# Writing the memory readout in runs of 64 elements, with a new instruction order, in a fused two-branch attention kernel

## The chip, the cores and the metric

The kernel runs on one core of one Trainium2 chip. The metric is the device time of one execution in microseconds (us); lower is better. Five engines run side by side, each working through its own list in order: TensorE (PE in the profile, with its weight loads as PEld), VectorE (DVE), ScalarE (ACT), GpSimd (POOL) and SyncE (SP, which here only starts DMAs). An instruction starts when the ones ahead of it on its engine have gone and the semaphores it waits for have been raised.

## The reference, cut to what matters

There are 2048 tokens, a model width of 640 and 32 heads of 20 features. Two attention branches, A and B, are mixed by a gate per token.

```python
# branch B, for each of 4 segments s of 512 tokens, per head
logits = qs @ ks.T * scale + mask          # causal inside the segment
a_dot  = softmax(logits) @ vs
num    = phi(qs) @ M                       # M, z: sums over the segments before
den    = phi(qs) @ z + 1e-6
o      = g * (num / den) + (1 - g) * a_dot # g = sigmoid(beta), per head
M, z   = M + phi(ks).T @ vs, z + phi(ks).sum(rows)
# branch A: phi_k = softmax features of k, kv = phi_k.T @ v, z = sum of phi_k
o      = (phi_q @ kv) / (phi_q @ z + 1e-6)
# result: gate = sigmoid(x . gate_w)
out    = gate * (oA @ A_wo) + (1 - gate) * (oB @ B_wo)
```

The division `num / den` is what the change rewrites. In the first segment M and z are zero, so the kernel computes it for segments 1 to 3 only: 12 token tiles of 128 tokens.

## The kernel before, in words

Tokens stand in 16 tiles of 128, or 4 segments of 512. Branch B's projections (line 627) give q and k with features on the partitions, and SyncE copies and transposes them through DRAM. The attention of a segment runs in 8 steps of 4 heads (b_step): scores on PE (L754), exponentials on ACT (L763), causal masks on POOL (L767), then the product with v (L795). Branch A's key side (a_k: L894, L901, L907 to L909) and running sum of features (L949) fill the first half of the program, its query side (a_q: L1003, L1008, L1020, L1055, L1060, L1064) and the output product (final: L1083, L1084) the second.

The memory readout sits in b_out. For each of the 12 token tiles PE forms numerator and denominator for all heads in one PSUM tile of two banks, 16 heads to a bank, 21 fp32 words per head: 20 of the numerator and the denominator behind them (L858, L859). VectorE takes the 32 denominators out (L864), inverts them (L867), and then, once per bank, multiplies 16 heads by 20 features with the inverse of their head (L869) and writes bf16 into an SBUF tile `mo`. A DMA transposes `mo` into `moT` (L468), and L877 adds `moT` to the other half of the output `oP`. `mo` is laid out as (c b h d), c being 5 groups of features and d 4 features within a group, because `oP` has its rows in that order; so the 320 elements of one L869 lie in 5 runs of 64.

Nothing in the program decides the order at run time. A table, ORDER, lists all operations in the order in which they are recorded; each engine's list is that order cut down to its own operations. CHOICE says, for the operations that two engines could do (mostly copies out of PSUM: ACT at L606 or VectorE at L607), which one does, and WHERE gives each tile its PSUM bank or SBUF slot. A tile that takes over a bank waits until the last reader of the bank's former tile is done. NSPIN is the number of idle matmuls (L1095) that the table places where it likes.

Of the kernel before, what the change touches and what calls it, by code (L numbers as in the profile page):

```python
# [36 lines left out]
om 3o p5 3p ow ox 47 7z os ph 4l 7s 4n ot 3a 4i 4m 7k 4j 17 7t p8 4o p9 4p 48 p0 oi oj 4r p1 19 4q dc 4u pq ou 4v pi p6 4w pr oy 4x 7l dd p7 oz pa ps
54 6z 70 7u 56 4s 55 oq f 4t 7v 57 dk 72 or p2 58 50 4y 51 qh 52 pj qi pk 4z pb 5c dl 73 53 59 5d pd pc 71 5e di 5v 5a pl pm 7o pn dj 74 pe pf 8t da
16 5x 5w 5l 5n pg 7p 5m po 85 8r 5o pv q1 75 db 5g q2 5i 10o 76 77 q6 5h pp 5j pw q7 q8 qb bx 5y 1f 5z 5f 5r qe 5k by 5t pt qf pu qc py 5s 5u qg 5p 67
pz q0 69 68 82 8u 4k 5q bw qd 60 8a 61 8s 6c 10p bz q9 8b 6d 8c px 63 6e 64 dg 65 q3 qa 6m 6o do 6f 6n 6a dp q4 dh ho hr q5 r1 8v qj qk 66 r2 r3 qs r4  # L40
6i r5 qt 8d 6b 6k 8e ds ql 6j 8f 6g qu 6h qv 90 c0 qm qn 6p qw dt 6l 1e hs qo 92 91 qp c1 qq c2 qr 8w 8x hp 6q qx 83 8g 8y 1d 8h 8i c4 rp rq qy rr 8z
6r 6s 95 96 dq qz dr 97 r0 rh 9f r9 ri 93 rj 9h 84 88 62 c3 87 89 ru 9g 8j rv 1c 8k 98 rk ra c5 dm 8l rl 94 rb 9i 9b 9c 9d 10q rm 86 9j rn 99 dn r6 c6
j8 rw 9a j9 a6 sk a7 r7 9e ro re rf 3q 9k j2 a8 9w sl a9 sm rc 9y rs 6t j3 9l 9x hq ht rd sf rt a2 sg sp a3 a4 e2 e3 e4 rg r8 s0 9n s3 s4 s5 s6 a5 10r
s2 1b 9p rx s1 rz aa 9r 9o 9t 9z 5b ry 79 s7 s8 t0 s9 sa 9s 9u ss t1 sq j4 9q t2 9m st sb su t5 t6 sx ab ax ac 1o j5 9v sc ay sd se sr a0 az t7 sy sn
a1 sz so sh e5 si e6 e7 ai sv ak sw de sj aj te at b0 j6 au av t3 ad j7 t4 ae hu ag jc df ja dw tf af tg b1 du th ti dv an ao hv tz tb ap jd aq tc aw
hw jb t8 e8 ta e9 ea t9 b2 td tj dx b3 ah tk b9 al tl tm ba u6 bb b5 u0 b7 b6 u1 b8 c7 u7 u3 u2 u4 u8 u9 1p 1a ua am uc dy ub ar 1q 1v 1x 1y 1w 1z 20
78 c8 bc c9 ud hx ue be tv bf bg as je eb tt jf u5 bo uf ec bq hy bp 3r ed ug bd bk tw bm bh bi bj bl hz el ei br ca i0 bn jg i1 es eu et tr bs ee jh
uh ui bt bu ju jv uj f3 f4 f5 jx jy jw 7a eo eq 8m uk e0 um ep uo un ev 3s ji jz ex ez ts tn ey k0 k1 k2 f6 ew ul 7b jj to 8n f0 8o up tp er 8p cq f7
ej cr cs ct f9 cu f8 d2 d3 7c d4 d5 d6 fa e1 f1 fj ck f2 7d fk fl fb dz cl cm cn co tx tu k3 cv fc tq k4 fy ur k5 fz g0 ef uq 7e jk fu fw v7 b4 em jl
v8 va bv fd v9 v2 cb v3 v4 ty fv ux 7f v5 uy 7h v0 cp us vc vb jm ce uz v1 cc vl vf vm vd vg vn ut vo 7g ve cd g1 vi cf cw fx vh uu vj uv vk vp cx cg  # L50
zf vq vr uw g2 cy d0 ka zg cz vs d7 ch d1 ci en i2 fo fp fq fr ek zc ff vt zd kd vu v6 fg fh fi zl zm jn g3 g4 vv gl gn vw vy gm w0 vx eg zi d8 cj d9
zj eh gp wr ii gr ij ik gq ws vz w1 wu wv wt ww jp ic id fe x0 x1 wx x2 wy wo wz ie ig fm fn fs iu wp wq im if il gf gh gg kb ft gs iv iw iy ix w3 go
ga gc w2 gb x3 x4 g6 g7 jo js gi in wj w9 g8 w4 wk wl wm w5 gt ze we ih g9 wa w6 w7 y9 ya yb y0 gu wc wf y6 wh wb y1 k6 y2 gx gv gy wn gz wg zx h1 kc
zy gd y7 y8 ge h0 gj gk w8 h2 h3 x5 h4 h6 h7 wd x6 hg wi hh h5 hi hj x7 h8 jt x8 zo hc y3 hd zk h9 ha zp kv he zu kw ke kf kx kz hb x9 i6 hk zv y4 y5
l1 l0 hf hl ky hm kp kq xb yc kr ks kk kl jr zr km yd l2 gw l3 kg ye l4 kh ki kn zq hn zs xc lb iz jq lc ld l7 l9 l5 l8 ko kj xa kt g5 la ku i3 i5 i7
lg lh lm lo zz li le i4 xd lq lr ls lf ln lj lt lp xe xf yf l6 yg lk mh mj mi i8 lu md mf me lv m7 m8 m9 m2 m4 m3 lw mk ml ly m0 lz i9 mg k7 ma mm m5
# [7 lines left out]
012345671014530143501034035310301053401354130100220132001210012313223010233001103231132200126327101642110267010435001200310260313321401321241305100262
310403031521012313202031230103203160207210230030103413521200111214331010211321340232110023213001201030100113221103201020132033220332023023131200232304
567010530100000530241025103410230023200332000031011260710122230021132331002041005210607114500136371000042310030812332034031302116004071514567212010130
000041063201340182004512303245032250031112260126270014201076021610201020601021600011230030000213003232003120300223820013030221306120101232003518021733
# [1105 lines left out]
```

## Time and profile before

| | us |
|---|---|
| median of 3 runs (338.68 to 341.3) | 340.35 |
| the profiled execution | 340.44 |
| its span, first to last instruction | 338.9 |
| mean granted TensorE clock | 0.919 |
| PE busy in the span | 293.3 |
| VectorE busy | 255.5 |
| ScalarE busy | 247.3 |
| GpSimd busy | 121.5 |

The profiled execution is the one that all rows come from; 1.5 us of its time lie around the span. Busy time of PE is modelled from the starts of pipelined matmuls. [...] The chain of waits is followed back from the last instruction: at each step to the instruction that released it, or to the one before it on its engine.

### The profile page before, as it was taken

The numbers are of one execution on the slowest core, as the hardware profiler recorded it, in microseconds if no ns is written. First come the engines' busy times: TensorE is split into PE (matmuls) and PEld (weight loads), VectorE is DVE, ScalarE is ACT, GpSimd is POOL, SyncE is SP. The second block draws the span as 40 slices with busy tenths as digits, with TensorE's granted clock in tenths as the row PEclk, the third lists the DMA queues.
The fourth block names the chain that finished last, engine by engine and source line by source line (L and its number), as shares of the span: only waits on it lengthen the run. The fifth ranks groups of instructions, "written<-read, shape, count | busy, mean of one in ns | idle before, by whom it ended". The sixth has DMA issues, their size and how long they took to land.

```text
span 338.9 us, 7011 instructions
## 1 busy us (share of the span) xinstructions
PE 293.3 (87%) x2882; PEld 152.0 (45%) x2882; DVE 255.5 (75%) x394; ACT 247.3 (73%) x323; POOL 121.5 (36%) x135
## 2 busy tenths in 40 slices
PE   2999999999989999999984999956988667695996
PEld 2354544565455464454542454424534223352653
DVE  2457587998999998999978987696552325989970
ACT  4476698989989999999995668774699989740001
POOL 4002733329645857843422104203142455330000
PEclk9999999999999999999998799995999855767899
DMA  7999470043136301061064776542762541397462
GB/s 218 247 213 206 61 153 3 22 68 71 33 53 123 79 10 42 33 151 41 21 184 128 201 148 92 124 128 45 106 166 75 168 144 48 88 193 173 80 183 90
DMA packets 72271, 37.38 MB, mean 110 GB/s; under 512 B 55184, under 2 KB 69168, under 8 KB 72240
## 3 DMA queue, kind: packets, MB, share of 16 engines
q1 hardware_dynamic: 71488, 36.08, 47.1%
q10 hardware_dynamic: 656, 0.82, 0.7%
q8 instruction: 23, 0.38, 0.5%
q0 software_dynamic: 96, 0.04, 0.2%
q14 instruction: 8, 0.07, 0.1%
HBM read 14.01 MB, written 12.10 MB: 77 GB/s over the span
## 4 chain that ended last, share of the span: by engine, by line
PE 53%; DVE 26%; ACT 12%; DMA 7%; issue 1%; SPq 0%; ACTq 0%
PE ps L627 9%; PE ps L1083 9%; DVE mo L869 8%; ACT expT L763 7%; PE ps L894 6%; DVE acc L949 4%; PE ps L754 4%; PE ps L1055 4%; PE ps L1003 4%; PE ps L795 3%; PE ps L649 3%; DVE z L907 3%; DMA stk<-in_B_wk_dram 2%; PE ps L1084 2%; ACT ej L763 2%; DMA acc<-acc 2%
## 5 line engine op out<-in xcount | busy, mean ns | idle before, releaser
L763 ACT ACTIVATE expT<-ps 128x1024 bf16<-128x1024 f32 x128 | 123.8, 1031 | 16.4 <-PE ps L754 15.6
L767 POOL TENSOR_SCALAR_AFFINE_SELECT expT<-expT 128x512 bf16<-128x512 bf16 x96 | 71.9, 760 | 119.8 <-ACT expT L763 105.4
L627 PE MATMUL ps<-xT,WB 128*128 128x512 bf16 x200 | 50.7, 388 | 1.0 <-DVE xT L607 0.6
L767 POOL TENSOR_SCALAR_AFFINE_SELECT ej<-ej 128x1024 bf16<-128x1024 bf16 x16 | 19.6, 1225 | 55.5 <-ACT ej L763 52.4
L763 ACT ACTIVATE ej<-ps 128x1024 bf16<-128x1024 f32 x32 | 31.4, 1030 | 6.8 <-PE ps L754 6.7
L869 DVE TENSOR_TENSOR mo<-ps,cs 128x320 bf16<-128x320 f32 x24 | 35.7, 1704 | 0.3
L1083 PE MATMUL ps<-Wo,oTA 128*128 128x512 bf16 x80 | 24.8, 395 | 5.1 <-DVE cs L864 3.0
L949 DVE TENSOR_TENSOR acc<-acc,E 64x1280 bf16<-64x1280 bf16 x31 | 27.7, 894 | 1.9 <-DMA acc<-acc 1.1
L1008 ACT ACTIVATE ET<-ps 128x512 bf16<-128x512 f32 x40 | 22.3, 602 | 8.1 <-PE ps L1003 7.6
L627 PEld LDWEIGHTS ps<-xT,WB 128*128 128x128 bf16 x200 | 17.6, 99 | 22.9 <-issue 4.5
L754 PE MATMUL ps<-qkm 20*128 20x128 bf16 (+3 forms) x320 | 21.1, 315 | 7.7 <-ACT expT L763 4.2
L795 PE MATMUL ps<-expT,v1B 128*21 128x384 bf16 (+2 forms) x384 | 27.2, 343 | 0.0
L606 ACT ACTIVATE out<-ps 128x640 bf16<-128x640 f32 x6 | 4.2, 703 | 31.0 <-PE ps L1084 31.0
L907 DVE TENSOR_REDUCE z<-E 128x64 f32<-128x1280 bf16 x16 | 23.6, 1475 | 3.4 <-ACT E L901 3.2
L909 POOL TENSOR_TENSOR E<-E,z 128x1280 bf16<-128x1280 bf16 x10 | 25.6, 2563 | 1.6 <-DVE MmI L534 0.8
L649 PE MATMUL ps<-WvB,xT 128*128 128x512 bf16 x80 | 25.2, 397 | 0.5 <-ACT eg L653 0.4
L901 ACT ACTIVATE E<-ps 128x640 bf16<-128x640 f32 x32 | 22.4, 708 | 3.8 <-PE ps L895 2.9
L1083 PE MATMUL ps<-Wo,oP 128*128 128x512 bf16 x80 | 24.5, 391 | 0.0
L1003 PE MATMUL ps<-xT,WqA 128*128 128x512 bf16 x100 | 23.6, 380 | 0.2 <-DVE oU L607 0.2
L894 PE MATMUL ps<-WkA,xT 128*128 128x512 bf16 x80 | 23.4, 380 | 0.4 <-ACT E L901 0.3
L607 DVE CAST oU<-ps 128x512 bf16<-128x512 f32 x22 | 15.0, 683 | 11.3 <-PE ps L795 11.2
L894 PE MATMUL ps<-WvA,xT 128*128 128x512 bf16 x80 | 23.2, 380 | 0.0
(130 smaller groups left out, 567.4 us busy)
## 6 DMA issues: line engine op xcount, KB each, us to landing
opk<-oU SPq DMA_DIRECT2D x16, 256.0 KB
oP<-opk SPq DMA_DIRECT2D x4, 640.0 KB
rx<-rc SPq DMA_DIRECT2D x16, 160.0 KB
...
```

Source lines behind the costliest of these rows:

```text
L627: r = e.matmul(self.pf(pt, 0, 0, LSEG), lhsT=self.WB[:, w, kc, 128 * c:128 * (c + 1)], rhs=xT[:, kc, LSEG * n:LSEG * (n + 1)], start=(kc = ...
L649: e.matmul(self.pf(pt, 0, 0, 512), lhsT=l, rhs=self.WvB[:, kc, 0:512], start=(kc == 0), stop=(kc == 4))
L754: r = e.matmul(self.pf(pts[i // 2], i % 2, c0, N), lhsT=view(32 * i, 32 * i + DH, 1, 128 * j, 128 * (j + 1)), rhs=view(32 * i, 32 * i + DH ...
L763: self.op("act", d_act(1024), lambda e, p=p, o=o: e.activation(o(), self.pbanks(pts[p], 0, 2, 512), ACT.Exp, scale=scale), W=[(pts[p], 0), ...
L767: self.op("pool", d_pool(n_el), lambda e: e.affine_select(view(), view(), pattern=pat, compare_op=ALU.is_ge, fill=0.0, base=0, channel_mul ...
L795: r = e.matmul(self.ps[32 * i:32 * i + 21, 512 * ad.t[0] + 128 * j:512 * ad.t[0] + LSEG], lhsT=vt[:, j, h, :], rhs=src[:, i, c0:c0 + N], s ...
L869: self.op("dve", d_dve(320, 1, True), lambda e, b=b, N4=N4, r=r, mo=mo: e.tensor_tensor(mo[:, :].rearrange("p (c b h d) -> p b h d c", b=2 ...
L894: e.matmul(self.pf(pt, 0, 0, 512), lhsT=l, rhs=W[:, kc, 0:512], start=(kc == 0), stop=(kc == 4))
L907: self.op("dve", 1.48, lambda e: e.tensor_reduce(z[:, :], Ev(), axis=AX.X, op=ALU.add), R=[(E, 0), (E, 1)], W=[(z, "*")], claim=[rz], pr=p ...
L949: self.op("dve", 0.9, lambda e, src=src: e.tensor_tensor(acc[lo:lo + 64, :], acc[lo:lo + 64, :], src(), ALU.add), R=[(self.Et[t], 0), (sel ...
L1003: r = e.matmul(self.pf(pt, 0, 0, LSEG), lhsT=self.WqA[:, kc, 128 * c:128 * (c + 1)], rhs=xT[:, kc, LSEG * S:LSEG * (S + 1)], start=(kc == ...
L1083: e.matmul(self.pf(pt, 0, 0, 512), lhsT=l, rhs=self.Wo[:, c, 0:512], start=(c == 0), stop=(c == 9))
```

## The change

The loops of L869 are exchanged. The output was walked head by head, feature by feature with the group c innermost, so that neighbouring elements of one write lay 128 elements apart; it is now walked group by group, so that 64 elements (16 heads by 4 features) are written in a row. What is written where is the same. The two inputs are walked in the same new order: the PSUM numerator was read in runs of 20 neighbouring words per head, and is now read with steps of 5 words (4 of them, then a hop to the next head); the inverse of the denominator was held for 20 elements, and now for 4.

The tables ORDER, CHOICE and WHERE are replaced as a whole, and NSPIN goes from 4 to 5. No duration in the code changes; the new durations that the title of the change speaks of stand only in the search that made the tables.

```diff
-NSPIN = 4
+NSPIN = 5
...
 ORDER = """
-6 4 v s t u w x 10 z y 8 5 2 7 9 d 3 a b 1i g 0 1j 1 k l o h p 1g m q j 1h n r 1m 11 2y 1l 2m 1n 2z 1k 2o 32 2n 2p 3y 33 21 3z 2q 2s 40 3u 15 2r 3v 3e
...
+5 6 4 0 8 1h 1g 11 1i 7 1 k m o 1j s i q 14 r 9 l d 12 13 1k j a p n 2u 1l h 2v 1m 2m 2n b 1n 2o 2p 2s g 3u v 6u 7s 7o 3v 3w 2q t u x 10 y w 3x z 7t
...
                     self.op("dve", d_dve(320, 1, True), lambda e, b=b, N4=N4, r=r, mo=mo: e.tensor_tensor(
-                        mo[:, :].rearrange("p (c b h d) -> p b h d c", b=2, h=16, d=4)[:, b], N4()[:, b, :, 0:DH].rearrange("p h (d c) -> p h d c", c=NCH),
-                        r[:, 16 * b:16 * b + 16].rearrange("p (h o u) -> p h o u", o=1, u=1).to_broadcast([128, 16, 4, NCH]), ALU.mult),
+                        mo[:, :].rearrange("p (c b h d) -> p b c h d", b=2, h=16, d=4)[:, b], N4()[:, b, :, 0:DH].rearrange("p h (d c) -> p c h d", c=NCH),
+                        r[:, 16 * b:16 * b + 16].rearrange("p (u h o) -> p u h o", o=1, u=1).to_broadcast([128, NCH, 16, 4]), ALU.mult),
                         R=[(r, "*")], W=[(mp, b), (mo, b)], pr=prq, name="memp")
```

Three places show what the tables move. The rows give line, operation and tiles; `cs` is the tile of denominators, `oA` branch A's output of a token tile, `qkm` a projection taken out of PSUM, `K1` branch A's summed keys and values. A number behind a tile's name is its buffer.

First, VectorE's list where segment 1's readout begins, in the middle of the program. Before:

```order
L864 TENSOR_SCALAR cs_119_205<-ps,iomg_75 128x32
L867 RECIPROCAL cs_119_205<-cs_119_205 128x32
L869 TENSOR_TENSOR mo_120_206<-ps,cs_119_205 128x64x5 x2
L864 TENSOR_SCALAR cs_121_207<-ps,iomg_75 128x32
L867 RECIPROCAL cs_121_207<-cs_121_207 128x32
L869 TENSOR_TENSOR mo_122_208<-ps,cs_121_207 128x64x5 x2
L830 TENSOR_TENSOR dc_84_170<-rqB_117_203,ps 128x128
L864 TENSOR_SCALAR cs_125_211<-ps,iomg_75 128x32
L867 RECIPROCAL cs_125_211<-cs_125_211 128x32
L869 TENSOR_TENSOR mo_126_212<-ps,cs_125_211 128x64x5 x2
```

And now:

```order
L864 TENSOR_SCALAR cs_116_202<-ps,iomg_75 128x32
L867 RECIPROCAL cs_116_202<-cs_116_202 128x32
L869 TENSOR_TENSOR mo_117_203<-ps,cs_116_202 128x5x64 x2
L607 CAST qkm1_57<-ps 128x512
L967 TENSOR_SCALAR zf_78<-ps 128x5
L968 COPY zf_78<-ps 128x5
L975 TENSOR_TENSOR K1_63<-KVZacc_61,Mk_70 128x8x20
L970 TENSOR_TENSOR K1_63<-Mk_70,zf_78 128x40 x2
L830 TENSOR_TENSOR dc_101_187<-rqB_118_204,ps 128x128
L607 CAST v1B1_60<-ps 128x32x20
L975 TENSOR_TENSOR K1_63<-KVZacc_61,Mk_70 128x2x7x20
L864 TENSOR_SCALAR cs_123_209<-ps,iomg_75 128x32
```

Three token tiles stood nearly one behind the other; now copies out of PSUM and branch A's summed keys stand between the first tile and the next.

Second, VectorE's list near the end, at segment 3's readout, where four writes of `mo` stood in a row. Before:

```order
L864 TENSOR_SCALAR cs_233_319<-ps,iomg_75 128x32
L867 RECIPROCAL cs_229_315<-cs_229_315 128x32
L867 RECIPROCAL cs_233_319<-cs_233_319 128x32
L869 TENSOR_TENSOR mo_234_320<-ps,cs_233_319 128x64x5
L869 TENSOR_TENSOR mo_230_316<-ps,cs_229_315 128x64x5
L869 TENSOR_TENSOR mo_234_320<-ps,cs_233_319 128x64x5
L869 TENSOR_TENSOR mo_230_316<-ps,cs_229_315 128x64x5
L864 TENSOR_SCALAR cs_238_324<-ps,iomg_75 128x32
L867 RECIPROCAL cs_238_324<-cs_238_324 128x32
L869 TENSOR_TENSOR mo_239_325<-ps,cs_238_324 128x64x5 x2
```

And now:

```order
L864 TENSOR_SCALAR cs_233_319<-ps,iomg_75 128x32
L1064 SCALAR_TENSOR_TENSOR oA_229_315<-ps,g_73,cs_230_316 128x320 x2
L864 TENSOR_SCALAR cs_235_321<-ps,iomg_75 128x32
L867 RECIPROCAL cs_235_321<-cs_235_321 128x32
L869 TENSOR_TENSOR mo_236_322<-ps,cs_235_321 128x5x64 x2
L867 RECIPROCAL cs_233_319<-cs_233_319 128x32
L869 TENSOR_TENSOR mo_234_320<-ps,cs_233_319 128x5x64 x2
L1040 TENSOR_TENSOR ET_183_269<-ET_183_269,rr_212_298 128x3x512
```

Two token tiles still follow each other, then branch A's work comes ahead of the last two tiles. In both orders the eight writes of segment 3 come near the end of VectorE's list, ahead of the last additions into `oP` (L877).

Third, SyncE's list near the start, where the load of WvA (branch A's value weights) stands. Before:

```order
L468 DMA_TRANSPOSE wqT_83<-in_A_wqkv_dram 128x5x640
L472 DMA ind<-MkF_69 128x5x32
L472 DMA WvA_53<-in_A_wqkv_dram 128x5x640
L468 DMA_TRANSPOSE kT_3_89<-qkm0_56 128x4x128
L468 DMA_TRANSPOSE xT_49<-in_A_x_dram 128x5x512
L468 DMA_TRANSPOSE kT_3_89<-qkm0_56 128x4x128 x3
```

And now:

```order
L468 DMA_TRANSPOSE wqT_83<-in_A_wqkv_dram 128x5x640
L468 DMA_TRANSPOSE kT_2_88<-qkm0_56 128x4x128
L472 DMA ind<-MkF_69 128x5x32
L468 DMA_TRANSPOSE kT_2_88<-qkm0_56 128x4x128 x4
L472 DMA WvA_53<-in_A_wqkv_dram 128x5x640
L468 DMA_TRANSPOSE xT_49<-in_A_x_dram 128x5x512
```

Five transposes of segment 0's keys, which wait for its projections, now stand ahead of the load.

CHOICE moves some operations between the engines. VectorE has 3 fewer copies of `out`, 3 fewer of `v1B`, 2 fewer of `qkm` and 1 fewer each of `xT`, `zs` and WkA, 4 more of `oU`, 3 more of `vA` and 3 more of WqA; ACT has the opposite. One normalization at L909 goes from VectorE (6, now 5) to GpSimd (10, now 11).

## Rows read from the trace of the kernel before

**Rows 1.** The page, engines: busy us, share of the span, instructions.

```profile
PE 293.3 (87%) x2882; PEld 152.0 (45%) x2882; DVE 255.5 (75%) x394; ACT 247.3 (73%) x323; POOL 121.5 (36%) x135
```

**Rows 2.** The page, chain of waits that ended last, by line.

```profile
PE ps L627 9%; PE ps L1083 9%; DVE mo L869 8%; ACT expT L763 7%; PE ps L894 6%; DVE acc L949 4%; PE ps L754 4%; PE ps L1055 4%; PE ps L1003 4%; PE ps L795 3%; PE ps L649 3%; DVE z L907 3%; DMA stk<-in_B_wk_dram 2%; PE ps L1084 2%; ACT ej L763 2%; DMA acc<-acc 2%
```

**Rows 3.** Chain in order of time: start us, us, what.

```profile
178.26 2.99 DVE mo L869 x2
...
220.32 5.85 DVE mo L869 x4
...
302.19 5.85 DVE mo L869 x4
308.48 2.99 DVE mo L869 x2
...
312.24 0.43 PE ps L1083
...
322.35 0.22 PE ps L1083
```

**Rows 4.** Waits: engine line waited for, us in total, times, longest.

```profile
PE ps L826 <- DVE cs L864: 3.4, 2, 2.5
PE ps L1083 <- DVE cs L864: 3.0, 1, 3.0
PE ps L1020 <- DVE mo L869: 2.7, 1, 2.7
PE ps L858 <- DVE mo L869: 2.4, 2, 2.1
PE ps L754 <- DVE cs L1060: 2.3, 1, 2.3
PE ps L754 <- DVE mo L869: 2.3, 1, 2.3
```

**Rows 5.** VectorE's groups: line, operation, shapes, count, busy us, mean ns, idle before.

```profile
L869 DVE TENSOR_TENSOR mo<-ps,cs 128x320 bf16<-128x320 f32 x24 | 35.7, 1704 | 0.3
L1064 DVE SCALAR_TENSOR_TENSOR oA<-ps,g,cs 128x320 bf16<-128x320 f32 x32 | 16.1, 544 | 0.4
L1060 DVE RECIPROCAL cs<-ps 128x32 f32<-128x32 f32 x16 | 5.5, 351 | 4.4 <-PE ps L1055 4.4
L867 DVE RECIPROCAL cs<-cs 128x32 f32<-128x32 f32 x12 | 4.1, 348 | 0.3
L864 DVE TENSOR_SCALAR cs<-ps,iomg 128x32 f32<-128x32 f32 x12 | 3.4, 285 | 3.7 <-PE ps L859 3.7
L967 DVE TENSOR_SCALAR zf<-ps 128x5 f32<-128x5 f32 x1 | 0.1, 142 | 0.0
```

**Rows 6.** Windows of 10 us: busy us (count) by engine, granted clock, DMA, GB/s.

```profile
180.00:190.00 10.00, 6.55 (x77) 3.16 (x78) 9.07 (x14) 3.35 (x6) 1.27 (x2) 0.66 0.45 136
220.00:230.00 10.00, 4.96 (x56) 2.07 (x53) 9.90 (x11) 7.46 (x12) 1.32 (x2) 0.87 0.42 110
230.00:240.00 10.00, 8.59 (x69) 5.67 (x70) 6.46 (x13) 2.54 (x4) 2.24 (x4) 0.62 0.38 80
250.00:260.00 10.00, 9.61 (x108) 4.56 (x107) 4.36 (x6) 9.07 (x12) 3.77 (x5) 1.00 0.31 89
280.00:290.00 10.00, 6.29 (x78) 2.89 (x70) 6.24 (x11) 8.88 (x10) 5.48 (x8) 0.56 0.13 41
300.00:310.00 10.00, 7.11 (x91) 3.96 (x89) 9.74 (x14) 1.90 (x3) 0.19 (x1) 0.84 0.81 173
310.00:320.00 10.00, 8.47 (x67) 5.28 (x68) 9.80 (x17) 0.71 (x1) 0.00 (x0) 0.69 0.60 124
```

**Rows 7.** Timeline: start us, us, engine, line, operation, tiles, count.

```profile
22.42 0.53 SPq L472 DMA_DIRECT2D WvA<-in_A_wqkv_dram  x1
...
29.48 3.83 SPq L468 DMA_TRANSPOSE kT<-qkm  x3
...
49.22 0.39 PE L894 MATMUL ps<-WvA,xT 128*128 128x512 bf16 x1
```

More of the change, by code (lines that the diff above doesn't have):

```diff
@@ L37 @@
[L37 to L56, printed above, removed]
@@ new lines @@
+2t 3y 2r 3z 40 15 6v 34 7p 7w 3e 21 28 7x 22 23 35 3f 2w 26 27 2x 7q 29 24 2a 7m 6w 41 42 3g 25 43 7r 7n 45 2b 44 6y 2g 2h 30 4d 46 4f 32 4e 2c 2d 33
+4g p3 p4 31 3h p5 p8 2 p9 6x c 49 4b 3i of e og 4a 3k 3j 2y 6z 2z 1r 3l on 3n 3m 2k oh 70 oo ok 39 op 1s oy 1t 2i 3o 3p 2l 2j 37 72 17 36 7i 2e 4h 1f
+4c oz 2f 38 7j 47 4l pa 7k 16 4m 3b 48 4n 4o 3d 7l os ov ow 4p ox ot 4r ou 4i dc 4j 3c ol 4q 4s 8q dd 3a om p6 p7 4u 4v 4t oi pq 4w 4x pr ps 19 oq p0
+oj 54 4y p1 55 or p2 80 50 ph 56 51 52 r4 81 4z 57 f 58 7u pe pi r5 pj pg 5c 53 59 pf 7v 7y 5d 5e 5l 5m 5n pk pl 10o 5a pb 7z 5g pc 85 pd 83 pv 5i 5o
@@ new lines @@
+3q 8a 18 5h 5v 8u 8b 8c 5f 5x qh 10p 5r 1u 73 pm qi 5w pn 74 4k dk 5s dl 5j 5k 5p 5t 6m 6n pw q1 q6 8t 6o q7 q8 5b q2 10q 5u 5y 5z 60 5q 61 6c 6e da
+10r 6d po 67 di pp 71 68 84 db py c0 bw px 6f bz 69 63 dj pz 6p q0 pt 6a 6b 82 6q qb 64 r1 65 pu q3 qc 6i q4 6k r2 by qe q5 qs 75 76 6j bx 6l qf qg q9
+dq qj qd 6r qa r3 8w c1 77 8d 66 8x 8y 88 dr dg qk 6s 8e 8f ql dh 90 91 92 c2 qt c4 do dp qu 1o 93 qm qo 6g 95 6h 96 94 97 ds qn 86 qp qv dt qw c3 qr
+8z 9f 9g qq 98 8g qx sk qy 9h c5 c6 8h 9i 8i 9b r6 9c r9 9d 1e 87 rk 3 qz ho ra r0 sl rh sm hq r7 8j rb ri rj 8r rp 9j 8v rl 9e 89 8k 8l rm 99 6t rq
@@ new lines @@
+hr 9k r8 8s rr 9n 9o rs 9p 9l de rt df hp 9a rn hs s3 9w e2 9x rc 9y dm e3 ro e4 9r rd sf j8 ru dn rv 9s sg re rf rw rg s4 s5 62 e5 9q 9t j9 dv ht a6
+s6 hu e6 s0 s7 a7 3r a8 hw e7 1c rx a2 s1 s2 sp 9z a9 sn s8 a4 sc ry a3 rz dx 9u 9v aa sq s9 so a0 a5 sd 7a se a1 ae j6 af ab j7 an ag ap ao j2 9m ac
+ss st sh si sj su dw sr j3 1p sa t0 ax ay t3 jc sb te az t1 ah t4 t2 jd e8 e9 1d ea tf at sx sv sy b0 au 1a t5 eb t6 b1 av ai sz t7 sw 1q t8 tg 79 ak
+t9 aw ec aq ed ta tb b2 aj b9 ba bb du th tc dy dz td b3 ti 1y e0 tr al 3s tj ad am 10s b5 b6 b7 tk tl tm u6 bc ar be bg uc as bf ud u7 tv hv 8m j4 bo
@@ new lines @@
+ue bq tt u3 bp u4 u9 ua u5 bh hx u0 20 u1 u8 1b je ub u2 j5 c7 b8 br bs bk uf bl 1v bd 1x hy 8n hz 1w ug jg bm bn bt ei 1z 78 jh c8 c9 ca i0 i1 es et
+eu jf 8o bu tz 8p bi ji bj eo cq jj ep ju tn eq uh ui ja uj uk 7b jv cr cs b4 ct ev cu jb jw f7 ew f9 to er tp ty bv f8 un fa tw tq um jx jy ex ul ez
+ey f0 uo tu 7c e1 7d jk jz d2 up cw tx k0 7e cx cy d3 cb cz d4 d6 d5 d0 k1 ts k2 f1 ur jl f3 ce k3 uq f2 cd f5 cf 7f v2 v3 v5 f4 k4 f6 d1 d7 k5 el v4
+v7 us ut cc fb ux vc vd ve vf vg vh jo uy uz v0 v1 vl vm cg vn vo vi vp vq uv vj vk fc v8 v9 7g va vb ck uu fy vr fz 7h g0 g1 ch cl cm cn co uw fo fp
@@ new lines @@
+vs fq vt ka zf fd fj ee ef i2 fk cp zl vu vv vw jn cv ci zg v6 fu cj fl d9 zc vz vy g2 zm fv ff fw d8 fr wu kd fh fx g3 zd fg gl zi wv ej gn gm gp fm
+ww gr gq g4 wr ws zj fn em go fi fs g6 g8 g7 gf gg gh jm wt ft wx x0 x1 ga gb gc x2 wo wp gs wy eg wq vx w0 w1 wz ek w2 w3 w4 gi eh en ic w5 w7 id w6
+zn gt gu h1 h3 h2 ie ig x3 if gx gz gy gd ge gv x4 jp jt g9 gj gk h4 we wf wg h6 w9 wh wi h7 wa wc h8 wj yc yd wk h9 y9 wb ye wd hg hh wl x5 wm w8 zu
+h0 k6 hi gw ya hc yb y6 zv h5 wn hj ha hb hd hk he hf kk y7 km kl fe zx zy y8 hl kp kq zo js kn hm kv zp kr x6 y3 kw x7 kx ky kz y4 l0 l1 zr y5 ks jq
@@ new lines @@
+jr zs kg kh ki x8 y0 y1 l2 y2 l3 l4 ko l5 ih iu lq lr ls kj kt zq ku iv iw ix iy l6 xc lm ln lo kb lp lg li lh xa l7 l8 l9 lt lu hn k7 k8 lb lc ld lj
+la lv m2 m4 m3 le lf ke io kf lw ip zw iq is ir ly lz xb x9 i6 lk m7 m0 m8 m9 g5 xd m5 i3 i5 i7 m6 i8 xe xf ma yf yg iz mh mj mi yh it ll yi xv md mf
+me xw xy xx m1 mb mc mk kc ml mg i4 mp mr mq yj yk xz mt mv mu mm mn ii my n0 mz k9 xq ij ik im zh lx il xr xs ze n8 n9 na mw xt xg n4 n5 n6 i9 yo xl
+ms mx n1 n2 yn ib ia n3 nb xh nc n7 xj nd xi ne xm mo yl ym in j1 j0 o1 o7 xu 106 107 yp o2 xo xn xk 100 101 o8 o9 oa ob o3 o5 o4 nf yq nj yr yx xp ng
@@ L63 @@
 WHERE = """
[L64 to L67, printed above, removed]
@@ L69 @@
+211310000021171301003243230235002023022113130723003020106214021726030021623010123010403015120067012000006101032312000212032222031300121513020031101028
+20133204310651010302108163122000023381172531346132
 """
```

14 lines of the change are left out of this document (6 added, 8 removed).

## The prediction, made before the changed kernel was run

> **What bounds the kernel now.** I read the page first, then the chain of waits, then the waits themselves, then VectorE's groups, and last windows of 10 us around the places that these named. PE is busy for 293.3 us, 87% of the span, VectorE for 255.5 and ACT for 247.3 [rows 1]: no engine is full from end to end, so the stages count. In the chain of waits the two largest lines are PE's, with 9% each, and the third is L869, the write of `mo`, with 8% [rows 2]; 8% of 338.9 us is 27 us. In order of time it stands there as pairs of 2.99 us and fours of 5.85 us, 18 of the 24 instructions in all, so one holds the chain for 5.85 / 4 = 1.46 us [rows 3] (its own 1.70 us overlap with the next one's start [rows 5]). The waits show who pays: PE stood idle for L869 itself, or for an instruction that had to queue behind it on VectorE (L864, L1060), for 3.4 + 3.0 + 2.7 + 2.4 + 2.3 + 2.3 = 16.1 us [rows 4]. All of it falls into stretches from 178 us on, where VectorE is busy for 9.07 to 9.90 us of 10, but for 230 to 240, and PE is not [rows 6]. The first 178 us hold no `mo` and are not touched by the exchanged loops.
>
> The same windows show a second cost. At 180 to 190, 230 to 240 and 310 to 320 us the granted clock is 0.66, 0.62 and 0.69, part of the stretch at the lower level, after PE had stood idle for VectorE. In the tail one L1083 holds the chain for 0.43 us at the lower level and, 10 us later, for 0.22 at the upper [rows 3].
>
> **The change, part by part.**
>
> *The exchanged loops.* The trace has no read of PSUM with steps of 5 words, so the new L869 has to be bounded. The nearest row is L1064: also 320 elements out of PSUM in fp32, also times 32 inverses held over several elements, also bf16 out; it writes in a row and reads 20 neighbouring words per head, and takes 544 ns against 1704 [rows 5]. What differs between that and the old L869 is above all the scattered write, so (1704 - 544) / 320 = 3.6 ns an element is its price, and 0.54 us is the low end for the new one. The other end comes from reads with hops: L864 takes 285 ns for 32 words that lie 21 apart, L967, the same operation on 5 adjacent words, 142 ns [rows 5]; if all of the difference is the hop, it is 143 / 27 = 5.3 ns an element, and the new L869 would take 0.14 + 320 x 5.3 ns = 1.84 us, more than now. Against that end: L1060 reads the same 32 hopping words as L864 and takes 351 ns, where L867 takes 348 on adjacent ones in SBUF [rows 5]; its 11 ns an element could hide a hop, but L864 also has a per-token factor that L967 has not. I take 0.65 us, near L1064, and keep 0.54 and 1.84 for the range. So each gives back 1.46 - 0.65 = 0.81 us: 24 x 0.81 = 19.4 us of VectorE, 18 x 0.81 = 14.6 us of the chain.
>
> The trace shows a scattered write at 1704 / 320 = 5.3 ns an element [rows 5]. [...]
>
> *What of it reaches the end.* PE's idle time behind L869 is the floor: 16.1 x 0.81 / 1.46 = 8.9 us. The chain is the ceiling: 14.6 us. The floor is too low because ACT, too, waits for scores that PE could not start; the ceiling too high because another wait may end only little sooner than L869 did. I take 12. Late next is PE itself: in 180 to 190, 230 to 240 and 300 to 320 us ACT is busy for only 3.35, 2.54, 1.90 and 0.71 us [rows 6] and does not wait to take over.
>
> *The clock.* PE's busy time times what the clock lacks of 1.00 is 6.55 x 0.34 + 4.96 x 0.13 + 8.59 x 0.38 + 7.11 x 0.16 + 8.47 x 0.31 = 9.9 us in the five windows with `mo` in or ahead of them (180, 220, 230, 300, 310) [rows 6]. I take half back, 5: the gaps of some 2.4 us at one wait [rows 4] would shrink to about 1, not to nothing. Ends: 0 and 9.9.
>
> *The new order.* It moves everything a little, and no row prices that. In the two readouts shown, copies and branch A's work now stand between token tiles; that helps only while `mo` is slow, since PE is fed by those copies, and costs nothing once it is short. At the start, WvA's load stands behind five transposes. It was issued at 22.42 us, its first use came at 49.22, and three of the transposes took 3.83 us [rows 7]: the slack of 26.8 us covers them, and if the projections are late by more than that, PE has other projections first. Zero for all of it, with ends of 6 us either way: two waits, of the longest kind that the trace has for VectorE (3.0 us [rows 4]), more or fewer.
>
> *Edits at nothing.* The operations that change engine take about 2 us from VectorE and give about 1 to ACT, which has its 1.9 us of work in 300 to 310 us [rows 6] as cover; without it they cost 1 us. GpSimd takes one more normalization and is busy for 36% [rows 1]. The fifth idle matmul costs about 0.2 us, what an L1083 of the same 512 columns takes at the upper level [rows 3].
>
> **Sum.** Against the profiled execution: 340.4 - 12 - 5 + 0 + 0.2 = 323.6, so **324 us**. The median of the runs shown is 340.35, the same to 0.1 us. With 8.9 to 14.6 for the waits, 0 to 9.9 for the clock and 6 either way for the order, the likeliest case has its own range of 316 to 332.
>
> **Rivals.**
>
> 1. *ACT takes over everywhere but in the tail.* For it: ACT is busy for 9.07 and 8.88 us in 250 to 260 and 280 to 290, the latter at a clock of 0.56 with PE waiting for exponentials; if the readouts before 300 us only reach that stretch sooner and wait there, what counts is the six instructions on the chain after 302 us [rows 3] and the clock behind them. Time: 340.4 - 6 x 0.81 - (1.1 + 2.6) / 2 = 333.7, so 334. Against: ACT is nearly idle right behind the readouts at 180 to 190 and 230 to 240 us [rows 6], so there it has room to take what PE sends sooner. Chance 0.17.
>
> 2. *The hop costs what the scatter cost.* A read at 4.1 ns an element makes the new L869 1.46 us, and nothing is gained: 340, within 2. For: L864's 5.3 ns at most. Against: L1060. Chance 0.08.
>
> 3. *Slower: the hopping read is dearer than the scattered write.* Place: the 18 writes of `mo` on the chain. It decides from 1.70 us a write on. At L864's 5.3 ns it is 1.84 us, 18 x 0.14 = 2.5 us, 343; if the whole of L864's 285 ns were its 32 reads, 8.9 ns each, it would be 2.85 us, 18 x 1.15 = 21 us, 361. I take 352 as its time. Against: L1060, and that an element would cost five times L1064's 544 / 320 = 1.7 ns. Chance 0.06. [...]
>
> 4. *More comes free.* The whole 14.6 us of the chain, all 9.9 of the clock, and 6 from the order: 340.4 - 30.5 = 310. For: the waits feed one another, since an idle PE loses clock and a slow PE delays ACT. Against: the gaps that DMA and ACT leave stay. Chance 0.14.
>
> That the loops are not exchanged in the built program is excluded: each of the 24 now stands with 5 x 64 elements in place of 64 x 5.
>
> **The numbers.** The likeliest case has 0.55, the rivals 0.17, 0.08, 0.06 and 0.14. A difference of about 1%, 3.4 us, can be told from none. Faster by more: 0.55, nearly all of the 0.17 and the 0.14, less a little where cases reach above 337: 0.82. Within 1%: most of rival 2 and bits of 1 and 3: 0.11. Slower: 0.07. The range from **312 to 337** leaves out rival 3, most of rival 2 and the lower half of rival 4, 0.06 + 0.07 + 0.06.
>
> **What would show it.** L869's mean should read 0.54 to 0.95 us in place of 1.70, and L869 should fall out of the chain's first lines. PE's waits on L869 and on what queues behind it should fall from 16.1 us to under 8. Granted clock in the stretches of the readouts should rise above 0.8. VectorE's busy time should be 226 to 236 us (255.5 - 2, less 24 times 0.75 to 1.16). Wrong would be: L869 above 1.4 us; or PE's idle time unchanged in sum, with ACT or DMA as its new cause; or a first half that grows longer by more than 3 us.

## The result: faster, but by half of what was forecast

| | before | changed |
|---|---|---|
| median beside each other, us | 340.63 (4 runs) | 331.34 (4 runs, 330.26 to 332.46) |
| ratio, 95% interval | | 0.9737 [0.9681, 0.9793] |
| span of the profiled execution, us | 338.9 | 330.3 |
| mean granted TensorE clock | 0.919 | 0.948 |

The forecast was 324 with a range of 312 to 337: the direction and the range hold, the size does not, 9.3 us gained where 16.8 were summed up. Every ratio here and below is of fast runs alone; one of the four runs with the loops alone, the one of 325.3 us, counts as slow, so it stands in that version's median and not in its ratio. First the page of the changed kernel, busy time by engine, which answers to [rows 1]:

```profile
PE 289.1 (88%) x2883; PEld 149.0 (45%) x2883; DVE 234.9 (71%) x392; ACT 247.8 (75%) x324; POOL 124.6 (38%) x136
```

VectorE lost 255.5 - 234.9 = 20.6 us. Its groups, against [rows 5]:

```profile
L1064 DVE SCALAR_TENSOR_TENSOR oA<-ps,g,cs 128x320 bf16<-128x320 f32 x32 | 16.0, 538 | 1.5 <-DMA moT<-mo 1.2
L869 DVE TENSOR_TENSOR mo<-ps,cs 128x320 bf16<-128x320 f32 x24 | 10.6, 482 | 0.3
```

L869 fell from 1704 to 482 ns, below L1064 and below the low end of 540 that the forecast gave it: reading PSUM with steps of 5 words costs nothing that can be seen beside L1064, which reads 20 in a row. The chain of waits in order of time (start us, us, what), against [rows 3], with the last pieces of the end of the program:

```profile
185.48 0.46 DVE mo L869
...
295.39 4.29 DMA opk<-oU
299.70 2.58 DMA dc<-opk
302.31 0.96 DVE rqB L820
304.34 0.74 DVE mo L869 x2
...
306.64 0.89 DVE mo L869 x2
...
308.50 2.62 DMA rrB<-rxB
...
313.49 0.69 DVE oP L877
314.32 0.58 PE ps L1083
315.01 0.43 PE ps L1083
```

Five writes of `mo` are in this listing of the longest pieces, where 18 were, for 2.1 us in place of 26.2; a sixth, of 0.19 us at 186.23, is too short for it. What now holds the end are the last segment's normalizers on their way through DRAM. TensorE's waits (engine, line, what it waited for: us, times, longest), against [rows 4]:

```profile
PE ps L1083 <- DVE oP L877: 4.7, 2, 3.1
PE ps L1055 <- DVE ET L1040: 3.2, 1, 3.2
PE ps L754 <- DVE oU L607: 2.8, 4, 1.0
...
PE ps L754 <- DVE mo L869: 1.6, 2, 1.1
PE ps L754 <- DVE vA L607: 1.6, 1, 1.6
...
PE ps L754 <- DVE cs L864: 0.4, 1, 0.4
```

For L869 and what queues behind it PE waits 1.6 + 0.4 = 2.0 us where it waited 16.1. New waits for other work of VectorE stand beside them. Windows of 10 us (busy us of PE, PEld, VectorE, ACT, POOL with counts, granted clock, DMA share, GB/s), against [rows 6]:

```profile
180.00:190.00 10.00, 8.80 (x108) 4.39 (x107) 6.01 (x19) 7.62 (x13) 1.79 (x3) 1.00 0.67 187
220.00:230.00 10.00, 8.13 (x94) 3.65 (x90) 5.59 (x11) 9.86 (x14) 3.52 (x6) 1.00 0.31 101
230.00:240.00 10.00, 8.76 (x121) 4.62 (x110) 7.84 (x19) 8.82 (x13) 3.98 (x6) 1.00 0.18 35
280.00:290.00 10.00, 8.60 (x100) 4.45 (x93) 7.76 (x16) 9.02 (x10) 4.48 (x8) 0.50 0.83 219
300.00:310.00 10.00, 10.00 (x111) 6.48 (x110) 7.74 (x19) 1.41 (x2) 0.00 (x0) 1.00 0.77 158
310.00:320.00 10.00, 6.93 (x54) 4.03 (x52) 6.22 (x11) 0.00 (x0) 0.00 (x0) 0.83 0.60 142
```

In the stretches that the forecast named the clock is back: 1.00 where 0.66, 0.87 and 0.62 stood, and 1.00 and 0.83 in the tail. The trace of before shows what the two levels of the prediction are: in windows of 1 us the clock reads 1.00 or 0.50, with values between them only where it changes, and the L1083 follow each other after 0.53 us at 0.50 (312 to 316 us) and after 0.27 at 1.00 (322 to 335 us). Four of its five falls, in the windows from 183, 227, 292 and 309 us, came during or up to 3 us behind a stretch with PE busy for 0.00 us (179 to 181, 224 to 226, 289 to 291, 309 to 311); the fifth, from 268, has PE busy for 0.24 of the microsecond ahead of it. The loss of 9.9 us in the five windows is down to 6.93 x 0.17 = 1.2. (From 260 to 300 us, of which the row from 280 is shown, it is 11.6 where it was 9.6.) Every step about the write came out, and yet 7 us of the forecast are missing. The term that the forecast put at zero, the new order, is the first place to look.

### The profile page after: what moved, and what is told of

The parts are those of the page before. It is cut to its first block, busy times and chain, and to the rows that moved or that the text cites. A ratio compares the mean times of both kernels' runs of the same rounds, so it can differ in the third digit from the quotient of the medians.

```text
span 330.3 us, 7013 instructions
## 1 busy us (share of the span) xinstructions
PE 289.1 (88%) x2883; PEld 149.0 (45%) x2883; DVE 234.9 (71%) x392; ACT 247.8 (75%) x324; POOL 124.6 (38%) x136
## 4 chain that ended last, share of the span: by engine, by line
PE 41%; DVE 21%; DMA 16%; ACT 11%; SPq 7%; issue 3%; POOL 0%; DVEq 0%
PE ps L627 9%; PE ps L1083 9%; ACT expT L763 7%; PE ps L1003 5%; DVE acc L949 4%; SPq L472 4%; PE ps L754 4%; SPq L468 3%; PE ps L795 3%; DMA dc<-opk 3%; DVE z L907 3%; PE ps L894 2%; DMA opk<-oU 2%; PE ps L1084 2%; DMA rrB<-rxB 2%
## 5 line engine op out<-in xcount | busy, mean ns | idle before, releaser
L763 ACT ACTIVATE expT<-ps 128x1024 bf16<-128x1024 f32 x128 | 124.5, 1030 | 20.8 <-PE ps L754 19.8
L763 ACT ACTIVATE ej<-ps 128x1024 bf16<-128x1024 f32 x32 | 31.2, 1040 | 3.0 <-PE ps L754 2.9
L909 POOL TENSOR_TENSOR E<-E,z 128x1280 bf16<-128x1280 bf16 x11 | 28.0, 2548 | 10.4 <-DVE z L908 9.4
L1083 PE MATMUL ps<-Wo,oTA 128*128 128x512 bf16 x80 | 24.8, 395 | 5.5 <-DVE oP L877 4.7
L754 PE MATMUL ps<-qkm 20*128 20x512 bf16 (+3 forms) x320 | 21.7, 322 | 8.5 <-DVE oU L607 2.0
L795 PE MATMUL ps<-expT,v1B 128*21 128x384 bf16 (+2 forms) x384 | 26.1, 342 | 2.6 <-POOL ej L767 1.2
L606 ACT ACTIVATE out<-ps 128x640 bf16<-128x640 f32 x9 | 6.2, 703 | 28.6 <-PE ps L1084 22.8
L607 DVE CAST oU<-ps 128x512 bf16<-128x512 f32 x26 | 17.7, 682 | 10.3 <-PE ps L795 10.2
L649 PE MATMUL ps<-WvB,xT 128*128 128x512 bf16 x80 | 23.9, 381 | 0.6 <-DVE M L716 0.5
L901 ACT ACTIVATE E<-ps 128x640 bf16<-128x640 f32 x32 | 22.1, 706 | 3.0 <-PE ps L895 2.5
L1083 PE MATMUL ps<-Wo,oP 128*128 128x512 bf16 x80 | 23.8, 383 | 0.0
L607 DVE CAST qkm<-ps 128x512 bf16<-128x512 f32 x24 | 16.2, 683 | 8.0 <-PE ps L627 7.9
```

The costliest lines, as they stand in the source:

```text
L607: return e.tensor_copy(o(), i())
L754: r = e.matmul(self.pf(pts[i // 2], i % 2, c0, N), lhsT=view(32 * i, 32 * i + DH, 1, 128 * j, 128 * (j + 1)), rhs=view(32 * i, 32 * i + DH ...
L763: self.op("act", d_act(1024), lambda e, p=p, o=o: e.activation(o(), self.pbanks(pts[p], 0, 2, 512), ACT.Exp, scale=scale), W=[(pts[p], 0), ...
L795: r = e.matmul(self.ps[32 * i:32 * i + 21, 512 * ad.t[0] + 128 * j:512 * ad.t[0] + LSEG], lhsT=vt[:, j, h, :], rhs=src[:, i, c0:c0 + N], s ...
L909: self.op(("dve", "pool"), {"pool": d_pool(1280, 2), "dve": 1.56}, lambda e: e.tensor_tensor(Ev(), Ev(), rz[:, :].rearrange("p (h o) -> p ...
L1083: e.matmul(self.pf(pt, 0, 0, 512), lhsT=l, rhs=self.Wo[:, c, 0:512], start=(c == 0), stop=(c == 9))
```

## The experiments

The theories: **A**, the loops give what was forecast and the new tables (ORDER, CHOICE, WHERE) give back some of it, mostly in the first 178 us; **B**, the tables cost nothing; **C**, the loops need the new tables. Every ratio below is against the kernel before on the same chip (339.6 to 340.4 us).

**The loops alone**: the tables of before, the new walk.

```diff
 (tables of before)
-... mo[...].rearrange("p (c b h d) -> p b h d c", ...)[:, b], N4()[...].rearrange("p h (d c) -> p h d c", c=NCH),
+... mo[...].rearrange("p (c b h d) -> p b c h d", ...)[:, b], N4()[...].rearrange("p h (d c) -> p c h d", c=NCH),
```

> The exchanged loops alone, on the tables (ORDER, CHOICE, WHERE, NSPIN) of before. Theory A (the loops give what was forecast, and the new tables give some 5 us back in the first 178 us, where TensorE was idle 4.8 us longer than before): the first 178 us stay as before, and the time is 322 to 327 us, faster than the changed kernel's 331.3. Theory B (the tables cost nothing; the loops are worth only some 9 us because other waits end little sooner): 330 to 333 us. Theory C (the loops need the new tables, which spread the writes): 334 to 338 us. In all three the write of mo has a mean of 0.48 us, as in the changed kernel.

Measured: **323.0 us** (320.26 to 325.3), ratio 0.9448 [0.9396, 0.95], span 322.5. By the medians that is 16.6 us off its kernel before (339.57), by the ratio 18.7; the forecast had 17 for waits and clock. This version beats the changed kernel. Its TensorE waits and, from the chain, its writes of `mo`:

```profile
PE ps L754 <- ACT expT L763: 8.1, 12, 1.3
...
PE ps L754 <- DVE mo L869: 0.5, 1, 0.5
...
PE ps L826 <- DVE mo L869: 0.4, 1, 0.4
...
PE ps L858 <- DVE cs L1060: 0.3, 1, 0.3
```

```profile
177.85 0.89 DVE mo L869 x2
179.32 0.89 DVE mo L869 x2
...
278.34 0.81 DVE mo L869 x2
...
289.48 1.40 DVE mo L869 x4
```

Even where four writes still stand in a row they hold the chain for 1.40 us, not 5.85. B and C fall.

**The tables alone**: the changed kernel with the old walk, the edit above turned round.

> The new tables alone, with the old scattered write of mo. Theory A: the tables lose some 5 us in the first half and the scattered writes stay, so 342 to 350 us. Theory B: 338 to 342 us, as before. Theory C (the tables bring part of the gain by themselves): 332 to 337 us. The write of mo has a mean of 1.70 us in all three.

Measured: 347.12 us (346.33 to 348.07), ratio 1.0214 [1.0176, 1.0251]: the tables cost 7.3 us without the loops by the ratio, and with them 331.3 - 323.0 = 8.3 by the medians, 9.8 by the ratios.

**What of the walk matters.** Two kernels walk L869 in another way in each of the segments 1 to 3. They serve for durations alone: the first in segment 2, the second in all three, leaves out that each numerator is taken from, or put into, its right place. The first, on the changed kernel's tables:

```diff
+ n == 1:  write "h c d" (4 neighbours, then a hop), read PSUM "h c d" (steps of 5 words)
+ n == 2:  write "c h d" (64 neighbours),            read PSUM densely, 320 words in a row
+ else:    write "d c h" (every 4th element),        read PSUM "d c h" (hops of 21 words)
```

> The changed kernel with another walk of the write of mo in each segment, to price it: segment 1 (8 writes) runs of 4 neighbouring bf16 elements, 16 x 5 x 4; segment 2 (8 writes) the 64-element runs of the change, but reading 320 neighbouring words of PSUM, so that its numerators are taken in the wrong order; segment 3 (8 writes) a write with steps of 4 elements and a read with steps of 21 words. If a hop in the PSUM read costs nothing, segment 2 takes 0.48 us, as the changed kernel; if the hop is what is left of the cost, 0.40 us or less. If a run of 4 is enough to write at full pace, segment 1 takes 0.48 us; if each hop costs, 64 of them per 256 elements, some 0.8 us. If any step of more than one element makes a write slow, segment 3 takes 1.7 us; if only a hop out of the neighbouring bytes does, less than 1 us.

It took 329.77 us (one run). Of tile `mo`: line, count, duration in ns (least, median, most), first and last start; L875, L877, L879 are the three walks in this order:

```profile
L875 DVE TENSOR_TENSOR mo<-ps,cs x8: 480/486/492, 180.1 to 202.7; 128x320 bf16<-128x320 f32 x8
L877 DVE TENSOR_TENSOR mo<-ps,cs x8: 480/486/492, 229.7 to 285.0; 128x320 bf16<-128x320 f32 x8
L879 DVE TENSOR_TENSOR mo<-ps,cs x8: 805/886/904, 294.7 to 305.3; 128x320 bf16<-128x320 f32 x8
```

Four neighbours in a row do as well as 64, and a dense read is no faster than steps of 5. The third walk hops on both sides, so a second kernel, on the tables of before, took the sides apart:

```diff
+ n == 1:  write 64 in a row,             read PSUM with hops of 21 words
+ n == 2:  write every 4th element,       read neighbouring words
+ else:    write every 128th element,     read neighbouring words
```

> The old tables, with L869 walked in a different way in each segment; the elements are not put where the reference wants them. Segment 1 writes 64 in a row and reads PSUM with hops of 21 words; segment 2 writes every 4th element (8 bytes) and reads neighbouring words; segment 3 writes every 128th element (256 bytes), as the kernel before, and reads neighbouring words, which no kernel did so far. If the write alone sets the duration: some 480 ns in segment 1, 890 in segment 2 (the walk that did both took 886), 1600 to 1800 in segment 3. If the long hop of the read costs what the every-4th write seemed to: 890 in segment 1 and 480 in segment 2. As a whole about 330, since a third of the writes is slow.

It took 328.45 us (one run); L875, L878 and L880 are the three walks:

```profile
L875 DVE TENSOR_TENSOR mo<-ps,cs x8: 480/486/493, 177.6 to 197.4; 128x320 bf16<-128x320 f32 x8
L878 DVE TENSOR_TENSOR mo<-ps,cs x8: 858/900/910, 214.8 to 278.5; 128x320 bf16<-128x320 f32 x8
L880 DVE TENSOR_TENSOR mo<-ps,cs x8: 1568/1793/1804, 290.4 to 303.8; 128x320 bf16<-128x320 f32 x8
```

In these forms the write alone sets the duration: 486, 900 and 1793 ns, whether the read is dense or hops.

**Where the tables cost.** Since each table lists operations nearly in order of time, two orders can be joined: the first so many operations of the one, then what is left in the order of the other. Tiles that then found their slot taken got another (one to six of them, by kernel). The walk is the new one in all of these. Each operation brings its engine (CHOICE) from the table that it comes from, and of the 62 operations that change engine 55 lie in the first 768 of the old order: what these kernels say of a stretch they say of order and choice of engine together, and no run took the two apart.

```diff
 old first, 178 us:  ORDER = old[:768] + the rest as in new
 new first, 178 us:  ORDER = new[:753] + the rest as in old
 old tail:           ORDER = new[:1200] + the rest as in old
```

> The exchanged loops, with the old tables' order for the first 768 of the operations (up to about 178 us, where segment 1's readout begins; four idle matmuls) and the new tables' order for the rest. Loops with old tables throughout took 323.0, with new tables throughout 331.3: the tables cost 8. Theory A (the first stretch costs most of it: TensorE waited 4.8 us longer there under the new tables): 326 to 328, and the first stretch's TensorE waits fall back to those of the kernel before. Theory D (lateness of the first stretch is made up later, since ScalarE sets the pace at 250 to 290 us, and the cost arises after 178 us): 330 to 332. Theory E (the loss is in the seam: an order fits only what it was searched with): above 333.

> The mirror image: the exchanged loops, with the new tables' order for the first 753 operations (up to about 178 us; five idle matmuls) and the old tables' order for the rest. Theory A: 326 to 328, with TensorE waiting some 9 us in the first stretch in place of 5. Theory D: 322 to 324. Theory E: above 333. Under A the differences of this run and of its mirror image from 323.0 and 331.3 should be the same size, 4 to 5 us.

> The exchanged loops, the new tables' order for the first 1200 operations (up to the last scores, about 289 us), and the old tables' order for what is left then. From the last scores to the end the old tables took 37.6 us and the new ones 41.0. Theory A with a tail (first stretch 4 to 5 us, tail 3 to 4): 327 to 328.5, with 37 to 38 us from the last scores to the end, because TensorE still has products of branch A to do while the last segment's normalizers travel by DMA. Rival F (the tail's length follows from what was left undone before it, so the new order's own leftovers decide): 330 to 333, the tail still 40 to 42 us.

| order | us | ratio |
|---|---|---|
| old throughout | 323.0 | 0.9448 [0.9396, 0.9500] |
| old to 178 us, then new | 325.06 | 0.9561 [0.9526, 0.9596] |
| new to 178 us, then old | 332.59 | 0.9790 [0.9747, 0.9832] |
| new to the last scores, then old | 334.96 | 0.9814 [0.9743, 0.9885] |
| new throughout | 331.34 | 0.9737 [0.9681, 0.9793] |

The stretch ahead of the first readout costs 331.3 - 325.1 = 6.3 us with the new rest behind it, and 332.6 - 323.0 = 9.6 with the old; the rest costs 325.1 - 323.0 = 2.1 behind the old first stretch and nothing behind the new one (331.3 against 332.6). (By the ratios the four are 6.0, 11.6, 3.8 and again nothing beyond the intervals.) The first kernel is under the 326 to 328 of A and far from D and E, so the first stretch costs most, more than the 4 to 5 expected. The second, 332.59, was to be 326 to 328 by A as well; it lies in no range, nearest to E, the seam, above 333, so that part of its 9.6 us may be the seam's. The third, 334.96, lies above the range of F (330 to 333), with 43.7 us from its last scores to the end where F had 40 to 42: the old tail brings nothing. That what is left over decides the tail fits the two kernels with the same new rest: behind the old first stretch its last scores start at 285.5 us and the span ends 38.0 us later (323.5); behind the new one they start at 289.3 and the end follows 41.0 us later. It is not the whole of it: with the old rest behind the new first stretch they start at 295.3 and the end follows 37.4 us later, so there the lag shows ahead of the last scores.

A look at one milestone would have missed this: the first readout starts at 176.6 us in the changed kernel, 177.0 before. The work done by then tells it. Sums of the windows from 0 to 178 us, before and then changed:

```profile
110.00:140.00 30.00, 29.41 (x292) 15.01 (x290) 28.39 (x36) 28.23 (x39) 22.51 (x15) 1.00 0.21 48
...
sum 178.00, PE 167.15 PEld 86.23 DVE 145.62 ACT 152.25 POOL 82.31; mean PE 33.43 PEld 17.25 DVE 29.12 ACT 30.45 POOL 16.46
```

```profile
110.00:140.00 30.00, 26.54 (x272) 13.94 (x270) 29.60 (x36) 25.46 (x37) 17.52 (x12) 1.00 0.47 98
...
sum 178.00, PE 161.90 PEld 84.26 DVE 144.76 ACT 145.60 POOL 84.53; mean PE 32.38 PEld 16.85 DVE 28.95 ACT 29.12 POOL 16.91
```

PE has done 5.3 us less and ACT 6.7 us less; VectorE, full in 110 to 140 us in both, about the same. ACT's exponentials up to 178 us, before and then changed (count, busy us, mean ns, idle time ahead of them):

```profile
L763 ACT ACTIVATE expT<-ps 128x1024 bf16<-128x1024 f32 x70 | 68.0, 1029 | 3.6 <-PE ps L754 3.0
...
L763 ACT ACTIVATE ej<-ps 128x1024 bf16<-128x1024 f32 x18 | 17.5, 1025 | 3.8 <-PE ps L754 3.7
```

```profile
L763 ACT ACTIVATE expT<-ps 128x1024 bf16<-128x1024 f32 x68 | 66.6, 1024 | 14.7 <-PE ps L754 14.3
...
L763 ACT ACTIVATE ej<-ps 128x1024 bf16<-128x1024 f32 x16 | 15.6, 1035 | 0.5 <-PE ps L754 0.4
```

84 where there were 88, and ACT waits 14.7 us for scores where it waited 6.7. Four of about 1.03 us are 4.1 us that the late stretch, where ACT is busy for 9.02 us of 10, has to take on.

**Which wait of the first stretch.** Three copies out of PSUM, for which PE waited 1.6, 1.0 and 1.0 us there, were moved up behind the products that they copy; and in another kernel four such copies went from VectorE to ScalarE.

```diff
 ORDER of the changed kernel, L607 on VectorE:
-... L735 pq, L607 vA          +... L607 vA, ... L735 pq
-... L735 pq, L607 oU          +... L607 oU, ... L735 pq
-... L937 KVZacc, L607 oU      +... L607 oU, ... L937 KVZacc
```

> The changed kernel with three of VectorE's copies out of PSUM moved up in the order, each to the place behind the product that it copies: one of vA (for which TensorE waited 1.6 us at 117.24 us) and two of oU (1.0 us each, at 120.10 and 158.05 us). Nothing else moves. Theory G (these waits themselves are what the new tables lose in the first stretch): the three waits go and 2.5 to 3.6 us come back, 327.5 to 329 against 331.3 of the changed kernel. Rival H (VectorE is busy without a break from 100 to 165 us, so what is put behind the copies comes later by as much and TensorE or ScalarE waits for that): 330.5 to 332.

Measured 333.05 us, ratio 0.9805 [0.9765, 0.9845]: no gain, theory G falls, and H's 330.5 to 332 is passed by 1 us. The waits came back under other names:

```profile
PE ps L754 <- DVE KVZacc L937: 2.0, 1, 2.0
PE ps L627 <- DVE oU L607: 1.4, 1, 1.4
...
PE ps L926 <- DVE qkm L607: 1.2, 1, 1.2
```

```diff
 CHOICE of the changed kernel, one vA_ev and three oU_ev:
-1 (VectorE, L607)
+0 (ScalarE, L606)
```

> The changed kernel with four copies out of PSUM between 100 and 165 us taken from VectorE and given to ScalarE, at the same places in the order: the copy of vA and three of oU, 2.8 us of VectorE's time (0.81 + 3 x 0.68). Moving three of them up on VectorE itself gave nothing (333.05). Theory J (in the first stretch the new tables leave VectorE too little room: it is busy without a break from 100 to 165 us, while ScalarE waits 14 us for scores): 327.5 to 329.5. Rival K (the order's lateness is not VectorE's room but what was begun too late; ScalarE's copies then push exponentials back): 331 to 334.

Measured 330.84 us, ratio 0.9708 [0.9658, 0.9759], inside the interval of the changed kernel. PE had done 1.2 us more by 178 us (163.1), but it did not reach the end. J (327.5 to 329.5) falls; the time is 0.2 us under K's lower end (331 to 334), so K is what it leaves, not what it shows.

**How early.** The old order was kept for shorter pieces, the new one put behind.

```diff
 ORDER = old[:466] + the rest as in new      (to about 110 us)
 ORDER = old[:589] + the rest as in new      (to about 140 us)
 ORDER = old[:215] + the rest as in new      (to about 50 us)
```

> The exchanged loops, the old tables' order for the first 466 operations (up to about 110 us), then the new tables' order. With the old order up to 178 us it took 325.1, with the new one throughout 331.3. If the new order loses its 6 us between 110 and 178 us, where TensorE's longest added waits stand (2.6 us at 110 to 130, 2.1 at 150 to 165), this takes 329 to 331; if it loses them earlier, where it puts more of branch A's work and fewer scores, 325 to 327; in equal shares 327 to 329.

> The same with the old order for the first 589 operations (up to about 140 us). If most of the 6 us is lost between 110 and 140 us: 325 to 327, with the run before it at 329 or more; if it is lost between 140 and 178 us: 329 to 331.

> The exchanged loops, the old tables' order for the first 215 operations (up to about 50 us), then the new tables' order. The old order up to 110 us gave 327.0 and up to 178 us 325.1; the new one throughout 331.3. If the loss sits in the start (the first projection begins 0.7 us later under the new tables, the first sum of features 9.3 us later, at 61.3 in place of 52.0 us): 326 to 328. If it arises between 50 and 110 us: 329.5 to 331.5. Above 333 would be a seam that fits badly, and would tell nothing.

To 110 us: **326.95**, ratio 0.9604 [0.9561, 0.9648]. To 50 us: 333.31, 0.9783 [0.971, 0.9855], nothing regained, but above the 333 from which on, as was said before it ran, a seam that fits badly would tell nothing; and PE is busy for less in it from 60 to 110 us (45.6 us) than in either order alone (48.9 before, 47.7 in the changed kernel). To 140 us: 333.34, 0.9808 [0.9777, 0.9838], but that seam made a wait of its own, which neither order has alone:

```profile
PE ps L627 <- ACT ej L763: 4.4, 1, 4.4
```

so this one tells nothing either. By the first, 331.34 - 326.95 = 4.4 us of the loss arise ahead of 110 us; how much of that ahead of 50 us stays open. By 110 us the new order is ahead on scores, 40 exponentials `expT` done by 110 us against 38, and behind on branch A's keys, 19 of their 32 exponentials (L901) against 23. That this exchange is the cause is what fits, not what was shown: no single operation was found whose place gives the time back.

One thing holds over all ten kernels with the new walk in every segment: the exponentials of L763 begun by 178 us go with the time. There are 89, 89 and 86 in the three fastest (323.0, 325.1 and 327.0 us) and 81 to 84 in the seven from 330.8 to 335.0. That bears out the measure, work done by a fixed time; it does not say what makes the lag.

## Why the prediction was right, and where it failed

*What bounds the kernel, and what pays:* right. L869 was the chain's third line, and without its scattered write PE's 16.1 us of waits are 1.4 in the version with the loops alone (0.5 + 0.4 + 0.3, and 0.2 for one L858) and 2.0 in the changed kernel. The 16.1 had left out two rows of the same kind, L754 behind L864 with 1.2 us and L858 behind L1060 with 0.2.

*The price of the new L869, 0.65 us:* right in its mechanism, too high in its size: 0.48. The nearest row, L1064, was the right neighbour; the end taken from L864 and L967, 5.3 ns for a hop in PSUM, was no hop price at all, as hops of 5 and of 21 words took 486 ns like a dense read, which for 320 elements are 1.5 ns an element with the fixed part in it. No run shows the 0.95 us that is the upper end among the signs, nor the 0.75 us a write that VectorE's 236 us rest on: L869 took 482 ns in the changed kernel, 1.22 us less than before.

*12 us for the waits, 5 for the clock:* right in sum, 17 against 16.6 with the loops alone (18.7 by the ratio), but that is luck: both parts are off and make up for each other. PE's waits on VectorE, summed over all rows of that view, fell from 21.1 to 8.0 us; those on ACT rose from 13.2 to 16.4, on DMA from 7.5 to 9.9 (3.2 of it for the transposes `oTA` in the tail), and 1.6 us came up for which the profile shows no cause: net 5.9 us, not 12, and less than the floor of 8.9. (That trace holds 2840 matmuls to 2882 weight loads where the one before has 2882 of each, so the 1.6 us may be matmuls missing from it; without them the net is 7.5.) The floor had left out that a wait which goes can come back on another engine. Rival 1 named that engine, ACT, and it did take over a part. The clock gave more. The loss, busy time times what is lacking from 1.00, was 9.9 us in the five windows and 9.6 in those from 260 to 300 us, 19.5; with the loops alone it is 9.3, of which 5.9 between 260 and 290 us, where ACT is busy for 8.08 to 9.39 us of 10, and 1.3 in the ten us behind, where PE waits for the transposes `oTA`:

```profile
230.00:240.00 10.00, 7.30 (x73) 3.48 (x72) 3.52 (x5) 8.60 (x10) 2.55 (x4) 0.87 0.58 139
...
260.00:270.00 10.00, 6.25 (x70) 2.06 (x66) 3.29 (x5) 8.08 (x10) 5.49 (x8) 0.60 0.49 155
270.00:280.00 10.00, 5.94 (x78) 2.85 (x82) 6.72 (x14) 9.39 (x11) 5.48 (x8) 0.66 0.13 41
280.00:290.00 10.00, 8.13 (x136) 5.61 (x130) 9.28 (x23) 8.33 (x10) 4.94 (x7) 0.83 0.74 171
```

So 10.2 us of clock, double the 5 that were taken, and 5.9 to 7.5 of waits: 16.1 to 17.7, beside the 16.4 by which the span is shorter. In the changed kernel the waits on VectorE stand at 19.6 us in sum: L869's went, others took their place; and the clock's loss over its whole span is 12.8 us, so that 3.5 of the 7.8 us between the two spans are clock.

*The new order, 0 with ends of 6 us:* this step failed, at a cost of 7 to 10 us (7.3 alone, 8.3 with the loops by the medians, and by the ratios 0.9737 - 0.9448 = 0.029 of 340, 9.8). It looked at the two readouts and at one load of the start, and took from them that the rest moves a little. The load was indeed harmless: issued at 35.30 us in place of 22.42, its first use came at 42.47, with no wait for it. But the first 178 us, of which the text said that the loops do not touch them, are what the tables change most, in a stretch where VectorE is full for most of the time and PE nearly so, and no row of it was costed. Two waits of 3 us were too narrow as ends: what counts is how much of ACT's and PE's work is behind at 178 us, and that was 6.7 and 5.3 us.

*The small edits:* VectorE's 234.9 us lie in the 226 to 236 that were forecast; the fifth idle matmul cannot be told from the rest.

*The rivals:* 2 and 3, a hop as dear as the scatter or dearer, are out with 482 ns. 1 came in part, as an engine that takes over, not with its 334. 4, 310 us, is out too: 323.0 was the least.

*The signs named ahead:* L869 at 0.54 to 0.95 us was missed to the good side; waits under 8 us and a clock above 0.8 in the readouts came true. Of the three that would show the forecast wrong none came as it was put: the first half did not grow longer, since the first readout starts 0.4 us earlier. Its loss of over 3 us stands in the work done by then.
